# The handover from attention to the first expert: two weight pieces, one copy and a row split put elsewhere

## The chip, the cores and the metric

The kernel runs on one core of one Trainium2 chip. The metric is device time in microseconds (us), as the median over runs of the whole program. The engines are PE (matrix products, with PEld for its weight loads), DVE (vector), ACT (scalar), POOL (GpSimd) and SP (which here only issues DMAs).

## What is computed

The reference is causal attention in a window of 64 positions (8 batches, 8 heads, 576 positions, head size 64), whose output rows (4608 tokens of 512) go through a mixture of 8 experts of which each token uses at most one:

```python
attn = softmax(mask(q @ k.T / 8)) @ v             # window of 64, causal
x = attn.transpose(0, 2, 1, 3).reshape(4608, 512)
do = x @ w_skip > 0                               # the other tokens stay x
e = argmax(x @ w_gate); g = softmax(x @ w_gate)[e]
out = x + g * (relu(x @ w1[e]) @ w2[e])           # where do
```

## The kernel before

**Attention.** The tokens are taken in 36 tiles of 128 (`NT`). For a tile t, `score` makes the scores on PE, `lessen` subtracts the maximum on DVE, `raise_e` is the exponential on ACT, `transpose_p` turns the result on PE and copies it out (`ptm`) on ACT, and `tile_out` multiplies by v (`av`), divides on DVE and stores the rows. The loop at L1182 covers tiles 0 to 34; what follows it (L1226 to L1286) drains the last tiles by hand while the first expert begins. The last tile, 35, is a tail tile: its v lies in `vt`, and `tail_lower(3, 1)` (L372, called at L1244) copies one block of v into place, 64 x 592 numbers on ACT.

**Routing.** The tiles are routed in groups of 8, 8, 6, 6 and 8 (`GRP`). The fourth group (tiles 22 to 27) and the last one (28 to 35) are what the change touches. For the last group `vector_part` (L427) splits the rows on DVE: sums of the gate values (`lg`), their maximum (`gmx`), the difference `gd` (L438), the chosen expert and the bf16 one-hot `gohb`, which PE multiplies with a triangle (`pr`, L513 and L516). `enter` and `one_hots` (L538, L574) then make list entries: some ten small operations on POOL (L581 to L591), two wider ones (L595, L596), a comparison on DVE (L600), two products on POOL (L611), then the list product `lp` on PE (L556). These are generators. `routes(1)` (L765) moves the first generator of queue `late` (the row split) one step on, then the first of queue `later` (the entries). At the marks "sums" and "lists" a generator is held for a count of calls, given by `HOLD`.

**Experts.** A weight piece is 128 x 1024 numbers of float32. SP loads it into one of 6 raw buffers (8 from L1299 on), `weight_hi` rounds it on ACT (`whi`), `weight_lo` subtracts (`wlo = raw - whi`, two inputs in SBUF, 128 x 1024), and the raw buffer is free again. Products are made of three terms (`mm3`). Pieces are counted from 0 here: 0, 1, 2 and 4 are the first expert's four quarters of w1, and 3, 5, 7 and 9 those of w2; 6 and 8 are the second expert's first two quarters of w1. Pieces 0, 1 and 2 are converted by hand, their `wlo` on POOL; all later ones in `weights_to`, on ACT and DVE. A raw buffer is loaded again by the next `weight_dma` in SP's order, which waits until the `wlo` that read it is done.

**Chunks.** `expert_chunks` cuts the products into chunks, and `expert_chunk` first converts weights and then issues the next chunk. With U for w1 and D for w2, a digit for the quarter and a, b for its halves, the chunks are: U0a, U0b, end; U1a, U1b, end; U2a, U2b, D0a, D0b, end; U3a, U3b, D1a, D1b, end; U4a, U4b, D2a, D2b, end; and so on (U4 is the second expert's). "End" chunks issue no products. A U chunk is 12 products into one of two PSUM buffers `p`, then `hh` on ACT and `hl` on DVE (L984, L987), which frees the buffer: so U1b needs the `hl` of U0b, U2a that of U1a, U2b that of U1b. A call of `routes(1)` follows each chunk. U2b and U3a also turn the second item's rows (L895).

**Order.** The kernel is scheduled by hand (`manual_schedule`): each engine takes its instructions in the order in which the program issues them. Before U0a the order is: tail copy on ACT, tile 34's output, turn of tile 35, piece 1 high and low, U0a, tile 35's output, piece 2 high and low, `routes`. Within a chunk the conversions come ahead of `hh` and `hl`. `need` at L1266 is what the next step uses; while routing goes on (`late`, `later` or `side` not empty), `weights_to` converts up to `need` at the first chunk of a step (two pieces together from piece 4 on).

Of the kernel before, what the change touches and what calls it, by code (L numbers as in the profile page):

```python
# [18 lines left out]
B, H, S, HD = 8, 8, 576, 64  # L19
# [3 lines left out]
NT = N // P  # L23
# [33 lines left out]
RATE = 1  # L57
# [1 line left out]
BOTH = 20  # L59
WAIT = {28: 6}  # L60
LWAIT = 8
HOLD = {"sums": 4, "lists": 4}

NXG = 9
CLOSED = 4 * S + 512
# [78 lines left out]
def window_attention_moe(ctx: ExitStack, tc, a, out):  # L144
    nc = tc.nc
# [12 lines left out]
    lists = dram.tile([LROWS, 2], I32, name="lists")  # L158
# [112 lines left out]
    def raise_e(t):  # L271
        s = ss[t]
        nc.scalar.activation(s, s, AF.Exp, scale=0.125)  # L273
# [13 lines left out]
    vms = {}  # L287
# [30 lines left out]
    def keep_busy(n):  # L318

        idle = pav.tile([P, 2, 512], F32, name="av")  # L320
        for _ in range(n):
            nc.tensor.matmul(
                idle[:, 0], onesb, onesb.unsqueeze(1).to_broadcast([P, 4, P]),
                start=True, stop=True, skip_group_check=True,
            )
# [44 lines left out]
        vs[9 * m + 8] = [vt[:, 0], vt[:, 1]]  # L370

    def tail_lower(m, z):  # L372
        nc.scalar.copy(vms["t", m][0][:64, z], vms[4 * m + 2 * z + 1][64:, 3])

    def av_tile(t, lh, sums, av=None):
        blks = tiles[t]
# [50 lines left out]
    def vector_part(t0, n, lh):  # L427
        lg = sm.tile([P, n, 9], F32, name="lg")
        nc.vector.tensor_reduce(lg, lh, axis=AX.X, op=ALU.add)
        l8 = lg[:, :, 0:E]  # L430
        sk = lg[:, :, E]
        g = nc.vector
        bc = lambda z: z.unsqueeze(2).to_broadcast([P, n, E])
        bn = lambda z: z.unsqueeze(1).to_broadcast([P, n, E])
        mx = sm.tile([P, n], F32, name="gmx")
        nc.vector.tensor_reduce(mx, l8, axis=AX.X, op=ALU.max)
        d = sm.tile([P, n, E], F32, name="gd")
        g.tensor_tensor(d, l8, bc(mx), op=ALU.subtract)  # L438
        yield
        fi = sm.tile([P, n, E], F32, name="gfi")  # L440
        nc.vector.scalar_tensor_tensor(fi, d, 0.0, bn(cf[:, off["rev"]]), op0=ALU.is_equal, op1=ALU.mult)
        nd = sm.tile([P, n], F32, name="gnd")
        nc.vector.scalar_tensor_tensor(
            nd, sk, 0.0, cf[:, off["oob"]][:, t0 : t0 + n], op0=ALU.is_le, op1=ALU.mult
        )
        ex = sm.tile([P, n, E], F32, name="gex")
        nc.scalar.activation(ex, d, AF.Exp)
        fm = sm.tile([P, n], F32, name="gfm")
        nc.vector.tensor_reduce(fm, fi, axis=AX.X, op=ALU.max)
        oh = sm.tile([P, n, E], F32, name="goh")  # L450
        nc.vector.tensor_tensor(oh, fi, bc(fm), op=ALU.is_equal)
        ohb = sm.tile([P, n, E], BF16, name="gohb")
        nc.vector.scalar_tensor_tensor(ohb, bc(sk), 0.0, oh, op0=ALU.is_gt, op1=ALU.mult)
        gs = sm.tile([P, n], F32, name="gs")
        nc.vector.tensor_reduce(gs, ex, axis=AX.X, op=ALU.add)
        g.tensor_scalar(gs, gs, 1e-9, None, op0=ALU.add)
        yield "sums"
        return nd, ohb, gs
# [253 lines left out]
    side, pace = [], [None]  # L712

    def drip():
        if side:
            job = side.pop(0)
            if job:
                job[0](*job[1:])
# [36 lines left out]
    late = []  # L755

    later = []
    held, held2 = [None, 0], [None, 0]

    def step(queue, h):  # L760
        h[:] = next(queue[0], queue), 0
        if h[0] is queue:
            queue.pop(0)

    def routes(n):  # L765

        for _ in range(n):
            for queue, h in ((late, held), (later, held2)):
                if not queue:
                    continue  # L770
                if h[0] in ("sums", "lists"):
                    h[1] += 1
                    if progress[0] < NT or h[1] < HOLD[h[0]] + (h is held2 and len(late)):
                        continue
                step(queue, h)

    def sums():
        step(late, held)
# [22 lines left out]
    progress = [0]  # L801

    steps = [(i, qi) for i in range(len(ITEMS)) for qi in range(NQ)]
    part = lambda k, w: (ITEMS[steps[k][0]][2], steps[k][1], w)
# [7 lines left out]
    when = {pc: n for n, pc in enumerate(pieces)}  # L812
    ring, used = [], {}
# [14 lines left out]
    RING = 9  # L828
    ptr = {"dma": 0, "split": 0, "free": 0, "use": 0}
    wrow = {}  # L830

    def weight_dma(n):
        e, qi, w = pieces[n]
        if e not in wrow:
            r = e % E
            ix = perm[0:1, r : r + 1] if r < 2 else tables["order"][0:1, r : r + 1]
            wrow[e] = nc.values_load(ix, engines=[SP], min_val=0, max_val=(E - 1) * NQ * P)
        raw_of[n] = idle.pop(0)
        nc.sync.dma_start(
            raw_of[n], a["wq"][bass.ds(wrow[e] + qi * P, P), w * 1024 : w * 1024 + 1024]  # L840
        )
# [5 lines left out]
    def weight_hi(n):  # L847
        nc.scalar.copy(ring[n % RING][0], raw_of[n])  # L848

    def weight_lo(n, by):  # L850
        hi, lo = ring[n % RING]
        by.tensor_tensor(lo, raw_of[n], hi.bitcast(F32), op=ALU.subtract)  # L852
        if not held_raw(n):
            idle.append(raw_of.pop(n))

    def weight_split(n):
        weight_hi(n)
        weight_lo(n, nc.vector)

    def weights_to(n):  # L860
        n = min(n, len(pieces), ptr["free"] + len(ring))
        while ptr["split"] < n:
            while ptr["dma"] < len(pieces) and idle:
                if not can_load(ptr["dma"]):
                    break
                weight_dma(ptr["dma"])
                ptr["dma"] += 1
            if ptr["dma"] == ptr["split"]:
                break
            weight_split(ptr["split"])  # L870
            ptr["split"] += 1
        while ptr["dma"] < len(pieces) and idle and can_load(ptr["dma"]):
            weight_dma(ptr["dma"])
            ptr["dma"] += 1
# [3 lines left out]
    def can_load(n):  # L878
        return pieces[n][0] % E < 2 or "order" in tables
# [259 lines left out]
    with tc.manual_schedule():  # L1139
# [31 lines left out]
        for m in range(B // 2):  # L1171
            z = 2 * (m == 0)
# [9 lines left out]
        for t in range(NT - 1):  # L1182
            m, r = divmod(t, 9)
            for f, n in at.get(t, ()):
                f(n)
            score(t + 1)
            gates = gate_at.get(t, ())
            if t == 0:
                keep_busy(5)
            for f, n in gates:  # L1190
                f(n)
            if t in (1, 2):
                transpose_p(t - 1)
            routes(1)
            if t != 3:
                lessen(t)
            raise_e(t)
            if t == 2:
                lessen(3)
            if BOTH <= t < NT - 3:  # L1200
                drip()
            if t >= 2:
                tile_out(t - 2)
            for f, n in after_at.get(t, ()):
                f(n)
            if t == NT - 2:
                weight_lo(0, nc.gpsimd)
            if t != NT - 3:
                drip()
            routes(1)  # L1210
            if t > 2:
                transpose_p(t - 1)
            if t == 1:
                clear_rows()
            if t == 7:
                load_constants()
            if t == 10:
                set_constants()
            routes(1)
            for f, n, j in lower_at.get(t, ()):  # L1220
                f(n, j)
            for _ in range(U0.count(t)):
                weight_dma_first()
            if t == NT - 3:
                weight_hi(0)
# [15 lines left out]
        pxs.append(psum.tile([P, 2, 2 * P], F32, name="px", tag="t", bufs=2))  # L1241
        turn_half(its[0].xg, pxs[1], 1)
        split_high(xhl[0][0], pxs)
        tail_lower(B // 2 - 1, 1)  # L1244
        drip()
        drip()
        split_low(*xhl[0], pxs)
# [1 line left out]
        tile_out(NT - 2, last_av)  # L1249
        routes(1)  # L1250
        transpose_p(NT - 1, turned)
        weight_hi(1)
        weight_lo(1, nc.gpsimd)
        scoring.close()
        moe = ExitStack()
        ml = moe.enter_context(tc.tile_pool(name="ml", bufs=1, reuse_waits="tile"))
        ring_slots(ml, 5 - NEARLY)
        hpool["h"] = ml
        chunks = expert_chunks()
        place = [0]  # L1260
        ptr["split"] = 2

        def expert_chunk():
            k = place[0]
            last = len(steps) - 1
            need = max(when[part(min(k + 1, last), 0)], when[part(min(k - 1, last), 1)] if k else 0) + 1  # L1266
            rate = 0 if late or later or side else RATE
            weights_to(max(need, min(ptr["split"] + rate, ptr["free"] + min(RING, len(ring)) - 1)))
            place[0], c = next(chunks)

        expert_chunk()
        drip()
        tile_out(NT - 1)
        weight_hi(2)
        weight_lo(2, nc.gpsimd)
        ptr["split"] = 3
        routes(1)
        pscore.close()
        banks["late"] = ctx.enter_context(tc.tile_pool(name="plate", bufs=1, space=PSUM, reuse_waits="tile"))
        for _ in range(2):  # L1280
            expert_chunk()
            routes(1)
            drip()
        attn.close()
        pattn.close()
        banks["v"] = ctx.enter_context(tc.tile_pool(name="plv", bufs=1, space=PSUM, side="right", reuse_waits="tile"))  # L1286
# [124 lines left out]
        while True:  # L1411
            k = place[0]
# [93 lines left out]
```

## Time and profile before

| what | us |
|---|---|
| median of 3 runs | 409.39 (408.86 to 409.62) |
| the profiled execution | 410.42 |
| its span, first to last instruction | 408.6 |
| PE busy / DVE busy / POOL busy in the span | 391.6 / 305.1 / 154.2 |

The profile is one execution; its rows give start and duration of each instruction in us from the span's start. "[1.30 <-DVE hl L987]" behind a row means that the engine stood idle for 1.30 us before it and that what came last was `hl`. Rows of the same kind that follow each other are merged (x2: two instructions, their stretch together). A PE row of several products overlaps the next row, since matmuls are pipelined.

### The profile page before, as it was taken

To read this page: it belongs to the slowest core of one execution; us is meant where nothing else is said; L and a number is where in the kernel's file an instruction comes from. 1 tells how busy PE (TensorE), PEld (TensorE's weight loads), DVE (VectorE), ACT (ScalarE), POOL (GpSimd) and SP (SyncE) were. 2 spreads that over 40 slices of the span, in tenths; PEclk is the share of its full clock that TensorE was granted. 3 is DMA by queue.
4 is the path that set the end of the run, shared out by engine and by line. 5 is a ranking of instruction groups with operands and counts; after the bars stand their busy time and mean duration, and the time that the engine had idled before them with its cause. 6 is when DMAs were issued, how large, how long until landed. Compare 5 with 4: busy or idle time off the path is not lost.

```text
span 408.6 us, 11475 instructions
## 1 busy us (share of the span) xinstructions
PE 391.6 (96%) x4624; PEld 327.7 (80%) x4624; DVE 305.1 (75%) x537; ACT 218.4 (53%) x373; POOL 154.2 (38%) x276
## 2 busy tenths in 40 slices
PE   8999999999999988899999999999999999999894
PEld 4777777787877778788888989988888888887773
DVE  3788799899899897999468698474375576758771
ACT  1778777866876786354243553442353544533440
POOL 5121368258568687976205042040043030100010
PEclk9999999999999999999999999999999999999898
DMA  8999999999994986847407959454337786642500
GB/s 296 406 400 373 407 408 404 412 389 367 394 341 161 303 280 212 268 157 227 147 2 221 352 161 298 150 181 146 104 117 232 256 276 209 232 135 71 186 31 23
DMA packets 34600, 99.41 MB, mean 243 GB/s; under 512 B 4368, under 2 KB 5648, under 8 KB 34544
## 3 DMA queue, kind: packets, MB, share of 16 engines
q1 hardware_dynamic: 30480, 87.30, 60.7%
q0 software_dynamic: 3200, 9.58, 6.8%
q10 hardware_dynamic: 864, 1.77, 1.1%
q8 instruction: 37, 0.61, 0.6%
q14 instruction: 19, 0.16, 0.1%
HBM read 84.57 MB, written 14.39 MB: 242 GB/s over the span
## 4 chain that ended last, share of the span: by engine, by line
PE 49%; issue 21%; DMA 12%; POOL 8%; DVE 6%; ACT 2%; SPq 1%; POOLq 1%; DVEq 0%
PE av L384 6%; DMA out<-yo,les 5%; PE p L921 5%; PE p L922 4%; PE p L923 4%; PE pt L281 4%; PE ps L252 4%; DMA vT<-vT 2%; DMA gid<-gid 2%; PE yw L921 2%; PE yw L922 2%; PE yw L923 2%; PE yv L921 2%; PE yv L922 2%; PE yv L923 2%
## 5 line engine op out<-in xcount | busy, mean ns | idle before, releaser
L852 DVE TENSOR_TENSOR wlo<-raw,whi 128x1024 fp32r<-128x1024 f32 x69 | 85.5, 1246 | 16.1 <-ACT whi L848 15.9
L984 ACT ACTIVATE hh<-p 128x256 fp32r<-128x256 f32 (+4 forms) x56 | 22.9, 409 | 97.0 <-PE p L923 92.8
L848 ACT CAST whi<-raw 128x1024 fp32r<-128x1024 f32 x72 | 74.4, 1044 | 0.0
L1024 POOL DMA_INDIRECT out<-yo,les x18 | 17.6, 976 | 146.3 <-DVE yo L1015 136.6
L921 PE MATMUL p<-xp,whi 128*128 128x256 f32 (+4 forms) x192 | 58.2, 303 | 1.0 <-DVE hl L987 1.0
L987 DVE SCALAR_TENSOR_TENSOR hl<-p,hh 128x256 fp32r<-128x256 f32 (+4 forms) x56 | 25.2, 451 | 44.7 <-ACT hh L984 33.0
L922 PE MATMUL p<-xp,whi 128*128 128x256 f32 (+4 forms) x192 | 57.0, 297 | 0.0
L923 PE MATMUL p<-xp,wlo 128*128 128x256 f32 (+4 forms) x192 | 56.8, 296 | 0.0
L273 ACT ACTIVATE s<-s 128x1024 f32<-128x1024 f32 x36 | 38.1, 1058 | 27.3 <-DVE s L268 27.1
L267 DVE TENSOR_REDUCE mx<-ps 128x8 f32<-128x1024 f32 x36 | 43.6, 1212 | 6.3 <-PE ps L252 6.3
L268 DVE TENSOR_TENSOR s<-ps,mx 128x1024 f32<-128x1024 f32 x36 | 44.1, 1225 | 4.8 <-PE pt L281 0.3
L384 PEld LDWEIGHTS av<-vm,ptm 128*64 128x64 f32 x992 | 34.3, 136 | 8.8 <-issue 5.9
L384 PE MATMUL av<-vm,ptm 128*64 128x74 f32 x992 | 39.0, 230 | 0.1
L921 PEld LDWEIGHTS p<-xp,whi 128*128 128x128 f32 x192 | 36.2, 188 | 3.7 <-DVE hl L987 1.4
L281 PE MATMUL pt<-gid,s 128*128 128x128 f32 x280 | 38.4, 279 | 0.1
L282 ACT COPY ptm<-pt 128x512 f32<-128x512 f32 x70 | 37.4, 581 | 1.4 <-PE pt L281 1.0
L922 PEld LDWEIGHTS p<-xp,whi 128*128 128x128 f32 x192 | 36.1, 188 | 0.7
L923 PEld LDWEIGHTS p<-xp,wlo 128*128 128x128 f32 x192 | 36.1, 188 | 0.0
L252 PE MATMUL ps<-k,q 64*64 64x128 f32 x1024 | 33.5, 269 | 0.0
L281 PEld LDWEIGHTS pt<-gid,s 128*128 128x128 f32 x280 | 30.1, 141 | 3.1 <-issue 0.4
L353 POOL COPY vm<-vm 64x1184 f32<-64x1184 f32 (+1 forms) x17 | 18.8, 1108 | 35.4 <-ACT vm L351 34.5
L252 PEld LDWEIGHTS ps<-k,q 64*64 64x64 f32 x1024 | 30.2, 133 | 2.1
(240 smaller groups left out, 826.1 us busy)
## 6 DMA issues: line engine op xcount, KB each, us to landing
raw<-wq SPq DMA_DIRECT2D x72, 512.0 KB, 4.7
vm<-vp SPq DMA_DIRECT2D x16, 592.0 KB, 8.2
vT<-vT SPq DMA_DIRECT2D x16, 512.0 KB, 7.6
out<-x SPq DMA_DIRECT2D x32, 256.0 KB, 6.2
q<-qT SPq DMA_DIRECT2D x13, 512.0 KB, 8.1
k<-kT SPq DMA_DIRECT2D x8, 640.0 KB, 8.1
k<-kT SPq DMA_DIRECT2D x7, 512.0 KB, 6.8
kt<-kT SPq DMA_DIRECT2D x8, 256.0 KB, 6.8
```

The costliest lines, as they stand in the source:

```text
L252: nc.tensor.matmul(ps[64 * hf : 64 * hf + 64, r, p], q[h, p], k[h, :, p], start=False, stop=p == 3, skip_group_check=True,)
L267: nc.vector.tensor_reduce(mx, flat, axis=AX.X, op=ALU.max)
L268: pace[0] = nc.vector.tensor_tensor(s, flat, mx.unsqueeze(2).to_broadcast([P, 8, P]), op=ALU.subtract)
L273: nc.scalar.activation(s, s, AF.Exp, scale=0.125)
L281: nc.tensor.transpose(pt[:, p], s[:, 4 * r + p], ident)
L282: nc.scalar.copy(ptm[:, 4 * r : 4 * r + 4], pt)
L384: nc.tensor.matmul(av[64 * hf : 64 * hf + 64, h // 4, (h % 4) * VW : (h % 4 + 1) * VW], ptm[:, (h % 2) * 4 + h // 2, 64 * hf : 64 * hf + 6 ...
L848: nc.scalar.copy(ring[n % RING][0], raw_of[n])
L852: by.tensor_tensor(lo, raw_of[n], hi.bitcast(F32), op=ALU.subtract)
L921: nc.tensor.matmul(o, lh, rh, start=first, stop=False, skip_group_check=parts)
L922: nc.tensor.matmul(o, lh, rl, start=False, stop=False, skip_group_check=parts)
L923: nc.tensor.matmul(o, ll, rh, start=False, stop=last, skip_group_check=parts)
```

## The change

- `weight_hi(1)` takes the place that the tail copy had on ACT, and `weight_lo(1)` goes to DVE behind tile 34's output.
- `weight_hi(2)` and `weight_lo(2)` (still POOL) are issued ahead of U0a, no longer behind tile 35's output.
- `tail_lower(3, 1)` goes to POOL, behind `weight_lo(0)` in the loop's last pass.
- In `vector_part` the difference `gd` moves behind the `yield`, into the next step: it is issued after U0b's `hl`.
- `routes` ends after the step that brings the row split to "sums", so that the entries take no step in that call; the call behind the first "end" chunk is left out; `HOLD["sums"]` is 3 in place of 4.
- While routing goes on, `expert_chunk` converts one piece at every second chunk of a step, as many as `need` asks, and at the least what the step itself uses.

```diff
-HOLD = {"sums": 4, "lists": 4}
+HOLD = {"sums": 3, "lists": 4}
     def tail_lower(m, z):
-        nc.scalar.copy(vms["t", m][0][:64, z], vms[4 * m + 2 * z + 1][64:, 3])
+        to, of = vms["t", m][0][:64, z], vms[4 * m + 2 * z + 1][64:, 3]
+        if m < B // 2 - 1 or z == 0:
+            nc.scalar.copy(to, of)
+        else:
+            nc.gpsimd.tensor_copy(to, of)
...
         nc.vector.tensor_reduce(mx, l8, axis=AX.X, op=ALU.max)
+        yield
         d = sm.tile([P, n, E], F32, name="gd")
         g.tensor_tensor(d, l8, bc(mx), op=ALU.subtract)
-        yield
...
                 step(queue, h)
+                if progress[0] == NT and held == ["sums", 0]:
+                    break
...
                 weight_lo(0, nc.gpsimd)
+                tail_lower(B // 2 - 1, 1)
...
         split_high(xhl[0][0], pxs)
-        tail_lower(B // 2 - 1, 1)
+        weight_hi(1)
...
         transpose_p(NT - 1, turned)
-        weight_hi(1)
-        weight_lo(1, nc.gpsimd)
+        weight_lo(1, nc.vector)
...
-        place = [0]
-        ptr["split"] = 2
+        place, turn = [0], [0, 0]
+        weight_hi(2)
+        weight_lo(2, nc.gpsimd)
+        ptr["split"] = 3
...
+            if k != turn[0]:
+                turn[:] = k, 0
             need = max(when[part(min(k + 1, last), 0)], when[part(min(k - 1, last), 1)] if k else 0) + 1
-            rate = 0 if late or later or side else RATE
-            weights_to(max(need, min(ptr["split"] + rate, ptr["free"] + min(RING, len(ring)) - 1)))
+            if late or later or side:
+                now = max(when[part(min(k, last), 0)], when[part(k - 2, 1)] if k > 1 else 0) + 1
+                weights_to(max(now, min(need, ptr["split"] + (turn[1] % 2 == 0))))
+            else:
+                weights_to(max(need, min(ptr["split"] + RATE, ptr["free"] + min(RING, len(ring)) - 1)))
+            turn[1] += 1
             place[0], c = next(chunks)
 
         expert_chunk()
         drip()
         tile_out(NT - 1)
-        weight_hi(2)
-        weight_lo(2, nc.gpsimd)
-        ptr["split"] = 3
         routes(1)
...
-        for _ in range(2):
-            expert_chunk()
-            routes(1)
-            drip()
+        expert_chunk()
+        routes(1)
+        drip()
+        expert_chunk()
+        drip()
```

## Rows read from the trace of the kernel before

**Rows 1.** Windows: us, busy time PE, PEld, DVE, ACT, POOL, clock, DMA.
```profile
158.40:186.70 28.30, 24.84 (x180) 22.25 (x177) 26.11 (x52) 12.49 (x21) 23.09 (x36) 1.00 0.64 209
186.70:362.00 175.30, 175.21 (x1156) 153.96 (x1155) 116.49 (x195) 76.23 (x129) 40.70 (x35) 1.00 0.60 194
```

**Rows 2.** Waits of PE from 150 to 186: us in total, times, longest.
```profile
PE p L921 <- DVE hl L987: 2.8, 3, 1.3
PE lp L556 <- POOL xg L611: 0.7, 2, 0.4
```

**Rows 3.** Timeline of PE: start, us, what, idle time before and its end.
```profile
162.96 0.39 PE L921 MATMUL p<-xh,whi 128*128 128x256 f32 x1 [1.30 <-DVE hl L987]
...
164.50 0.20 PE L513 MATMUL pr<-gohb,trib 128*128 128x64 bf16 x1
...
165.43 0.39 PE L921 MATMUL p<-xh,whi 128*128 128x256 f32 x1 [0.53 <-DVE hl L987]
...
166.96 0.32 PE L921 MATMUL p<-xh,whi 128*128 128x256 f32 x1
...
169.48 0.44 PE L556 MATMUL lp<-xg,xg 128*128 128x160 bf16 x4 [0.42 <-POOL xg L611]
...
181.78 0.39 PE L921 MATMUL p<-xp,whi 128*128 128x256 f32 x1 [0.96 <-DVE hl L987]
...
183.29 0.73 PE L556 MATMUL lp<-xg,xg 128*128 128x160 bf16 x8
```

**Rows 4.** Timeline of DVE around the first expert.
```profile
158.00 0.42 DVE L987 SCALAR_TENSOR_TENSOR hl<-p,hh 128x256 fp32r<-128x256 f32 x1 [1.57 <-ACT hh L984]
...
160.94 1.63 DVE L438 TENSOR_TENSOR gd<-lg,gmx 128x64 f32<-128x64 f32 x1
162.50 0.41 DVE L987 SCALAR_TENSOR_TENSOR hl<-p,hh 128x256 fp32r<-128x256 f32 x1
...
163.33 0.25 DVE L451 TENSOR_TENSOR goh<-gfi,gfm 128x64 f32<-128x64 f32 x1
...
164.09 0.95 DVE L600 TENSOR_TENSOR xg<-cf,gk 128x768 bf16<-128x768 f32 x1
164.95 0.42 DVE L987 SCALAR_TENSOR_TENSOR hl<-p,hh 128x256 fp32r<-128x256 f32 x1
165.29 1.22 DVE L852 TENSOR_TENSOR wlo<-raw,whi 128x1024 fp32r<-128x1024 f32 x1
...
170.05 2.46 DVE L852 TENSOR_TENSOR wlo<-raw,whi 128x1024 fp32r<-128x1024 f32 x2
...
177.77 3.61 DVE L852 TENSOR_TENSOR wlo<-raw,whi 128x1024 fp32r<-128x1024 f32 x2
```

**Rows 5.** Timeline of POOL in the same stretch.
```profile
157.76 4.74 POOL L852 TENSOR_TENSOR wlo<-raw,whi 128x1024 fp32r<-128x1024 f32 x2 [1.20 <-ACT whi L848]
...
167.37 0.71 POOL L596 TENSOR_SCALAR xg<-xg 128x192 f32<-128x192 f32 x1
168.16 1.95 POOL L611 TENSOR_TENSOR xg<-xg,vals 128x640 bf16<-128x640 f32 x2
170.06 1.37 POOL L533 TENSOR_TENSOR gds<-gds,gohb 128x64 f32<-128x64 f32 x1
...
178.66 3.85 POOL L611 TENSOR_TENSOR xg<-xg,vals 128x640 bf16<-128x640 f32 x2
```

**Rows 6.** Timeline of ACT: tail copy, last tile's turn, piece 1, and U0b's `hh`.
```profile
154.37 0.69 ACT L373 COPY vt<-vm 64x592 f32<-64x592 f32 x1
155.53 0.59 ACT L282 COPY ptm<-turned 128x512 f32<-128x512 f32 x1 [0.48 <-PE turned L281]
...
156.63 1.05 ACT L848 CAST whi<-raw 128x1024 fp32r<-128x1024 f32 x1
...
160.16 0.38 ACT L984 ACTIVATE hh<-p 128x256 fp32r<-128x256 f32 x1 [1.26 <-PE p L923]
```

**Rows 7.** Groups of POOL by form: the like of the moved copy.
```profile
L353 POOL COPY vm<-vm 64x592 f32<-64x592 f32 x2 | 1.3, 670 | 8.9 <-ACT vm L351 8.9
```

## The prediction

> **What bounds the kernel now.** Read the windows first: from 186.7 to 362 PE is busy for 175.21 of 175.30 us, at full clock; in the 28.3 us before that, 158.4 to 186.7, it is busy for 24.84, and DVE for 26.11 [rows 1]. So a microsecond by which the products of the first expert end sooner is carried to the end, as long as the work behind it (loads, conversions, row gathers, which are chained to PE through `hl` and `wlo`) comes along; and PE's idle 3.46 us of that stretch are all that there is to gain there. The waits name them: 2.8 us in three waits for `hl` on DVE, 0.7 in two for the entries' products on POOL [rows 2]. The timeline of PE places them: 1.30 before U1b at 162.96, 0.53 before U2a at 165.43, 0.42 and the rest of the 0.7 at the list product at 169.48, 0.96 before U4b at 181.78 [rows 3].
>
> DVE's timeline then says why [rows 4]. U1b needs the `hl` of U0b. Its `hh` is written by 160.54 [rows 6], but DVE first does `gd`, 64 numbers a partition, for 1.63 us; an operation of that shape takes 0.25 (`goh`). `gd` ends at 162.57, and POOL's two `wlo`, which began at 157.76 and took 4.74, end at 162.50 [rows 4, 5]. The other way round, POOL's `L533` on 64 numbers took 1.37 from 170.06, when DVE's two `wlo` began at 170.05 [rows 4, 5]. So an operation of DVE with two inputs in SBUF and one of POOL wait for each other's end. The Trainium skill has this as a rule (SBUF — State Buffer, Who interferes with whom): a DVE instruction with two SBUF inputs contends with a GpSimd one that reads SBUF, whichever starts first holds the port for the whole instruction, and a `tensor_reduce` never contends. The rows above agree; what the rule says against this change is taken up in the rivals.
>
> **Piece 1.** One `wlo` leaves POOL (half of 4.74, 2.37) and one comes to DVE (1.22 by the row at 165.29). DVE stood idle for 1.57 before 158.00 [rows 4], that is from 156.43, just where it is put; it ends about 157.65, ahead of the `hl` of U0a. Cost: nothing; without that cover it would be up to 1.2 on the `hl` chain. `weight_hi(1)` on ACT takes the place of the tail copy, 1.05 against 0.69; started at 154.37 it ends at 155.42, and ACT's next operation began only at 155.53, after 0.48 of waiting [rows 6].
>
> **Piece 2.** `weight_hi(2)` now stands where `weight_hi(1)` stood, ahead of U0a's `hh`, so ACT is unchanged there. POOL starts that `wlo` when it had started piece 1's, 157.76, and ends at 160.1 in place of 162.50; if DVE's new `wlo` holds up the small row operations of group four ahead of it, by up to 1.2 later, 161.3. On SP the load into the raw buffer of piece 2 now stands ahead of the store of tile 35, which then waits for POOL until 160 to 161; nothing reads those rows before the gathers of the third item, behind the second list product.
>
> **Tail copy on POOL.** 0.67 us for its like [rows 7], behind piece 0's `wlo`. Behind it on POOL stand the second item's two gathers, read first by the turn after U2b, and the row sums of group four. Tile 35's v is there four microseconds ahead of its use. Cost between 0 and 0.67 on POOL, none on PE.
>
> **`gd` behind the `hl` of U0b.** That `hl` now starts at 160.94, where `gd` had, and ends at 161.35. PE came free at 161.66 (162.96 less 1.30) [rows 3], so U1b starts there: 1.30 gained. Even if `gd` still meets POOL's `wlo`, it no longer stands ahead of this `hl`.
>
> **Up to U2a.** U1b to the triangle product takes 1.54 (162.96 to 164.50), that product 0.40 (to 165.43 less 0.53): PE is at 163.20 and 163.60. On DVE `hl`, `gd` at 0.25, the rest of the split (164.09 less 162.50 less 0.34, in which an `hl` makes room for the next, as from 164.95 to 165.29: 1.25) end at 160.94 + 0.34 + 0.25 + 1.25 = 162.78, since the entries' comparison no longer follows in that step. The `hl` of U1a then ends at 163.20 [rows 4], so U2a starts at 163.60 without a wait: 0.53 more. Gained so far 1.83. HOLD at 3, with one call left out, puts the triangle product in the same place, behind U1b.
>
> **U2b, a new wait.** The comparison (0.86 to the next start), piece 3's `wlo` (1.22) and the `hl` of U1b (0.42) now stand behind that `hl`: 163.12 + 0.86 + 1.22 + 0.42 = 165.62 [rows 4]. U2a ends at 163.60 + 1.53 = 165.13 [rows 3]. So U2b waits 0.49; if POOL's L596 (0.71 [rows 5]) gets in between, 1.20. I take 0.7, between the two, because POOL reaches L595 and L596 about when DVE reaches the comparison, and DVE may well be first. Gain at U2b: 1.13.
>
> **First list product.** The entries' steps come one chunk later and the product two chunks later, behind D0b. POOL starts them at about 161 in place of 162.58 and needs, as before, some 7.5 us (162.5 to 170.11 [rows 5]), to 168.5; D0b ends at about 170.7. The 0.67 of waiting goes; below nothing is excluded, as the product itself only moves. Gain 1.80.
>
> **Spread conversions.** Of pieces 4 to 9 the second of each pair comes two chunks later. Before U4b the `hl` of U3b stood behind both of pieces 6 and 7, which took 3.61 in place of 2.46 because POOL's two products (3.85) ran against them [rows 4, 5]. Now piece 6 alone is ahead of it: it is done by about 176.2, U4b starts about 178.5. The 0.96 goes. Gain 2.76. What is late next is piece 7 for D2a: behind the last group's comparison, with one POOL product of about 1.0 let through, I get its end at 180.1 and D2a at 180.4; and the second list product at 181.9, whose POOL part ends about 181.1. Both margins are below 1, so each may cost between 0 and 1.0; I take 0, as POOL and DVE both begin their part earlier than before.
>
> **Sum.** 1.30 + 0.53 - 0.70 + 0.67 + 0.96 = 2.76, say 2.8. The profiled execution took 410.42 with a span of 408.6 (1.8 lies around it); it is 1.0 above the median. Its like would take 407.6; from the median 409.39 the forecast is **406.6**. Bounds: U2b's wait at 0.49 gives 406.4; at 1.20 with 0.5 lost at D2a or the second list product 407.6. The forecast's own range is 406.1 to 407.7.
>
> **Rivals.**
> - *The port keeps DVE the bound* (408.0, chance 0.17). The rule of the Trainium skill above would have it so: the two engines still take turns, only elsewhere. From the rows: DVE has 26.11 busy of 28.3 and 2.2 idle [rows 1]; if only `gd`'s excess (1.63 less 0.25, 1.4) is saved and every other excess comes back with another partner, the stretch can shrink by 1.4. For: DVE is busier than PE there. Against: the excess in `wlo` (1.15) came from two conversions back to back.
> - *More than forecast* (405.6, 0.05): no wait at U2b, and other products start closer together; 3.46 idle plus small change.
> - *The waits come back* (409.4, 0.08): U2b at 1.20, D2a and the second list product 1.0 each leave 0.3, too little to measure. This is also where it ends if the edits move waits and remove none.
> - *Slower, by piece 7 too late* (410.6, 0.06). Before, piece 7 was ready at 181.38 and D2a followed U4b and the list product at 183.8. Now it stands right ahead of the product that needs it. If it ends after 183.8, three microseconds later than I get, all is lost, and each further turn of POOL's 1.0 on DVE is a loss; two such turns and a late pair of pieces 10 and 11 (1.2 more, since they are converted together once routing is over) give 1.2 slower. Against: POOL would have to be let in four times.
>
> **Chances.** Forecast 0.64, rivals as above. The range 405.7 to 408.7 takes in the forecast's own, the first and second rival's, and leaves out about 0.17. A measurement of this kernel can tell about 0.2%, 0.8 us, from no change: faster by more 0.85, within 0.09, slower 0.06.
>
> **What would show it.** Right: `gd` at about 0.25 behind `hl`; no idle time before U1b, U2a, the first list product and U4b; some 0.5 to 1 before U2b; D-chunks of the first expert some 2 us earlier, and PE dense from about 184. Wrong: `gd` or another small DVE operation above 1 us on the way to an `hl`; waits before D2a or the second list product; or new idle time behind 184, above all for a `hl` behind pieces 10 and 11, which would mean that the gain of this stretch is given back.

## The result and the profile after

| what | before | after |
|---|---|---|
| median, runs of one chip (us) | 409.50 (408.81 to 410.37, 6 runs) | 405.92 (405.52 to 406.51, 6 runs) |
| ratio, 95% interval | | 0.9915 [0.9900, 0.9931] |
| the profiled execution / its span | 410.42 / 408.6 | 405.84 / 404.1 |

The change gains 3.58 us, 0.85%; the forecast was 2.8. A second measurement of the same kernel on another chip (`after_again`, below) gave less, 2.87 by its medians, with a ratio of 0.9936 [0.9915, 0.9958]. The windows come first, as in [rows 1]: us, busy time of PE, PEld, DVE, ACT, POOL, clock, DMA, here of the kernel after, with the later edges moved roughly with the work.

```profile
158.40:183.70 25.30, 24.66 (x184) 22.44 (x183) 22.61 (x48) 11.29 (x19) 20.47 (x34) 1.00 0.72 237
183.70:357.50 173.80, 173.71 (x1145) 152.37 (x1145) 116.80 (x195) 76.61 (x130) 42.98 (x37) 1.00 0.60 197
```

PE's idle time in the first stretch fell from 3.46 [rows 1] to 0.64, by 2.82; behind 183.7 PE is as dense as before. The waits of PE from 158 to 200 (us in total, times, longest) have one line left:

```profile
PE p L927 <- DVE hl L993: 0.6, 1, 0.6
```

The timeline of PE after (start, us, what, idle time before and its end) answers to [rows 3]. From the top: U0a, U1b, the triangle product, U2a, U2b, U3a, U4b, the second list product, and the third item's first turn, behind the end of the stretch.

```profile
155.21 0.36 PE L927 MATMUL p<-xh,whi 128*128 128x256 f32 x1
...
160.96 0.28 PE L927 MATMUL p<-xh,whi 128*128 128x256 f32 x1
...
162.40 0.20 PE L517 MATMUL pr<-gohb,trib 128*128 128x64 bf16 x1
...
162.68 0.38 PE L927 MATMUL p<-xh,whi 128*128 128x256 f32 x1
...
165.02 0.38 PE L927 MATMUL p<-xh,whi 128*128 128x256 f32 x1 [0.64 <-DVE hl L993]
...
170.17 0.36 PE L927 MATMUL p<-xh,whi 128*128 128x256 f32 x1
...
177.77 0.28 PE L927 MATMUL p<-xp,whi 128*128 128x256 f32 x1
...
181.97 0.73 PE L560 MATMUL lp<-xg,xg 128*128 128x160 bf16 x8
...
195.32 0.49 PE L901 MATMUL px<-gid,xg 128*128 128x128 f32 x3
```

The rows of the kernel before that [rows 3] lacks for the comparison, from its timeline of PE: U0a, the product of U1a that first reads piece 1's `wlo`, the last product ahead of U1b's wait, U1b's second product (the first is in [rows 3]), U3a, and the third item's first turn.

```profile
155.64 0.36 PE L921 MATMUL p<-xh,whi 128*128 128x256 f32 x1
...
160.21 0.39 PE L923 MATMUL p<-xh,wlo 128*128 128x256 f32 x1
...
161.39 0.28 PE L923 MATMUL p<-xh,wlo 128*128 128x256 f32 x1
...
163.19 0.28 PE L922 MATMUL p<-xl,whi 128*128 128x256 f32 x1
...
173.13 0.28 PE L921 MATMUL p<-xh,whi 128*128 128x256 f32 x1
...
199.31 0.49 PE L895 MATMUL px<-gid,xg 128*128 128x128 f32 x3
```

From start to start the two traces compare like this (us; the forecast is the prediction's term, each taken from an idle row):

| from, to | before | after | gained | forecast |
|---|---|---|---|---|
| U0a to U1b | 7.32 | 5.75 | 1.57 | 1.30 |
| U1b to U2a | 2.47 | 1.72 | 0.75 | 0.53 |
| U2a to U2b | 1.53 | 2.34 | -0.81 | -0.70 |
| U2b to U3a (first list product within) | 6.17 | 5.15 | 1.02 | 0.67 |
| U3a to U4b | 8.65 | 7.60 | 1.05 | 0.96 |
| U4b to the third item's turn | 17.53 | 17.55 | -0.02 | 0 |
| sum | 43.67 | 40.11 | 3.56 | 2.76 |

The sum is the difference of the medians (3.58) to 0.02, which is closer than two executions of one kernel agree: in `after_again` the way from U0a to the third item's turn took 41.66, a gain of 2.01. The spans differ by 4.5, and the rest belongs to these two executions. U0a stood 0.43 earlier from work ahead of the change. Near the end the clock of PE differed: in the kernel before the granted clock fell to 0.73 and then 0.50, the level of 1.2 GHz, from 380 to 384, and in the kernel after the same work, four microseconds earlier, was done at 1.00. The windows (columns as above; before, then after):

```profile
380.00:382.00 2.00, 1.35 (x7) 1.35 (x7) 1.34 (x5) 1.17 (x2) 0.00 (x0) 0.73 0.28 91
382.00:384.00 2.00, 2.00 (x8) 1.71 (x7) 1.93 (x4) 0.45 (x2) 0.00 (x0) 0.50 0.00 0
```
```profile
376.00:380.00 4.00, 3.28 (x30) 2.46 (x30) 3.27 (x8) 1.60 (x4) 0.00 (x0) 1.00 0.14 47
```

The shift between the two traces is 3.99 at the third item's turn, still 3.98 ahead of these windows (the product at 380.65 before and 376.67 after), and 4.42 at PE's last product (402.80 and 398.38). So what the change gained was carried to the end, and 0.44 came on top there. Why the clock fell in the one execution and not in the other is not shown.

DVE's timeline after answers to [rows 4]: piece 1's `wlo`, U0b's `hl`, `gd`, the comparison, piece 3's `wlo`, the `hl` of U1b and of U2a, and piece 7's `wlo`.

```profile
155.84 1.22 DVE L858 TENSOR_TENSOR wlo<-raw,whi 128x1024 fp32r<-128x1024 f32 x1
...
160.39 0.41 DVE L993 SCALAR_TENSOR_TENSOR hl<-p,hh 128x256 fp32r<-128x256 f32 x1
160.72 0.21 DVE L443 TENSOR_TENSOR gd<-lg,gmx 128x64 f32<-128x64 f32 x1
...
162.54 0.95 DVE L604 TENSOR_TENSOR xg<-cf,gk 128x768 bf16<-128x768 f32 x1
163.41 1.22 DVE L858 TENSOR_TENSOR wlo<-raw,whi 128x1024 fp32r<-128x1024 f32 x1
164.54 0.75 DVE L993 SCALAR_TENSOR_TENSOR hl<-p,hh 128x256 fp32r<-128x256 f32 x2
...
176.73 1.41 DVE L858 TENSOR_TENSOR wlo<-raw,whi 128x1024 fp32r<-128x1024 f32 x1
```

`gd` takes 0.21 where it took 1.63 [rows 4], and stands behind the `hl`. POOL's timeline after answers to [rows 5]: the moved copy, a small sum, piece 2's `wlo`, an operation on 6 numbers, and the two pairs of entry products.

```profile
152.56 0.67 POOL L377 COPY vt<-vm 64x592 f32<-64x592 f32 x1 [0.44 <-DMA xg<-out,es]
...
156.03 1.16 POOL L537 TENSOR_TENSOR gds<-gds,gohb 128x48 f32<-128x48 f32 x1
...
158.32 2.40 POOL L858 TENSOR_TENSOR wlo<-raw,whi 128x1024 fp32r<-128x1024 f32 x1
...
163.63 1.05 POOL L595 TENSOR_TENSOR gl<-gl,vals 128x6 f32<-128x6 f32 x1
...
166.28 2.72 POOL L615 TENSOR_TENSOR xg<-xg,vals 128x640 bf16<-128x640 f32 x2
...
177.62 2.87 POOL L615 TENSOR_TENSOR xg<-xg,vals 128x640 bf16<-128x640 f32 x2
```

Piece 2's `wlo` ends at 160.72, ahead of `gd`'s row; the small operations that DVE's `wlo` holds up are now POOL's (1.16 and 1.05), and PE waits for none of them.

### The profile page after: what moved, and what is told of

Same layout as the page of the kernel before. It is cut to its first block, busy times and chain, and to the rows that moved or that the text cites. A ratio compares the mean times of both kernels' runs of the same rounds, so it can differ in the third digit from the quotient of the medians.

```text
span 404.1 us, 11475 instructions
## 1 busy us (share of the span) xinstructions
PE 389.3 (96%) x4624; PEld 325.4 (81%) x4624; DVE 303.6 (75%) x538; ACT 217.7 (54%) x372; POOL 154.8 (38%) x276
## 4 chain that ended last, share of the span: by engine, by line
PE 54%; issue 19%; DMA 12%; DVE 7%; POOL 5%; ACT 2%; SPq 1%; POOLq 0%; DVEq 0%
PE av L388 7%; PE p L927 5%; DMA out<-yo,les 5%; PE pt L281 5%; PE p L928 5%; PE p L929 5%; PE ps L252 4%; PE yw L927 2%; PE yw L928 2%; PE yw L929 2%; DMA gid<-gid 2%; PE yv L927 2%; PE pw L331 2%; PE yv L928 2%; PE yv L929 2%
## 5 line engine op out<-in xcount | busy, mean ns | idle before, releaser
L858 DVE TENSOR_TENSOR wlo<-raw,whi 128x1024 fp32r<-128x1024 f32 x70 | 86.5, 1240 | 16.2 <-ACT whi L854 16.0
L273 ACT ACTIVATE s<-s 128x1024 f32<-128x1024 f32 x36 | 38.1, 1058 | 27.4 <-DVE s L268 27.1
```

## The experiments

A ratio is to the kernel before on the same chip. Its median was 409.70 beside `gd_back`, `entries_back`, `pairs_back` and `odd_turns`, 411.03 beside `one_on_pool`, `gd_only`, `spread_only` and `tail_back`, 410.45 beside `late_three` and `after_again`, and 410.03 beside `both_back`; so times of different sets are compared by their ratios. "The distance" is the time from the last exponential (ACT L273) to the third item's first turn: 47.50 before, 43.88 after. In the second execution of the kernel after (`after_again`) it was 44.90, so a distance alone tells nothing below 1 us, and verdicts rest on the waits as well.

**What freed U1b.** Three kernels undo one of the two reasons, or both: POOL done earlier (piece 1 on DVE), and `gd` behind the `hl`.

`gd_back`, the kernel after with

```diff
-        yield
         d = sm.tile([P, n, E], F32, name="gd")
         g.tensor_tensor(d, l8, bc(mx), op=ALU.subtract)
+        yield
```

> The changed kernel with one part undone: gd is issued ahead of the hl of U0b again. If the gain before U1b came from POOL letting the port go earlier (its wlo of piece 2 ended at 160.72, gd would start at about 160.4), gd takes 0.3 to 0.6 us, U1b waits less than 0.7, and the time is 406.3 (405.9 to 406.8; changed kernel 405.9). If the order of gd and hl is what counted, gd is again above 1 us, U1b waits 1.3, and the time is about 407.4.

Measured: 406.17, ratio 0.9912 [0.9895, 0.9928], distance 43.85. `gd` began at 162.14 and took 0.30, for POOL's `wlo` (159.96, 2.40) ended at 162.36. There was no idle row before U1b, and 0.47 before U2b. With POOL done early the order of `gd` costs a quarter of a microsecond at most (U1a to U1b took 1.68, after 1.43).

`one_on_pool`, the kernel after with

```diff
-        weight_lo(1, nc.vector)
+        weight_lo(1, nc.gpsimd)
```

> The changed kernel with piece 1's wlo on POOL again, ahead of piece 2's. POOL's two then end at about 161.7, gd (from 160.7) waits for the port to 161.7, and the hl of U1a and everything DVE does behind it come 0.9 later: U2a and U2b 0.9 later, 406.7 (406.3 to 407.1). If it is enough that gd stands behind the hl of U0b, 405.9.

Measured: 408.37, ratio 0.9918 [0.9888, 0.9948], distance 44.90. Apart from a later start the trace is as expected: POOL's two `wlo` (158.87, 4.75) ended at 163.62 and `gd`, behind the `hl`, took 1.04, to 163.70. U1b had no idle row, but the triangle product waited 0.30, U2a 0.33, U2b 0.64, and from U1b's start U2a came 0.98 later than after. The distance equals that of `after_again` and the interval takes in the kernel after, so the size is not settled by this run.

`both_back` undoes both.

> The kernel after with two of its parts undone together: gd stands ahead of U0b's hl again, and piece 1's wlo is on POOL again. Each part alone undone left U1b without an idle row (gd met POOL's wlo for 0.30 and 1.04 us, in the one case because POOL had only one wlo left, in the other because gd stood behind the hl). If either of the two is enough and the pair is what frees U1b, gd now meets the first of two wlo on POOL again, takes about 1.6 us ahead of the hl, and U1b waits about 1.3 as before; the other parts keep their gains (no wait at U4b, list products without a wait). From U0b's start to the third item's first turn 38.9 to 39.5 us (after 37.3 and 38.0 in two executions, one_on_pool alone 38.6, before 40.9); time about 407.4. If U1b's wait had another cause, that distance stays at 37.3 to 38.6, the time at 406 to 406.7.

Measured: 407.73, ratio 0.9939 [0.9918, 0.9960], from U0b to the third item's turn 38.83, 0.07 below what was expected. The ratio is that of `after_again` (0.9936), so the verdict rests on the rows. From its timelines of PE, DVE and POOL:

```profile
162.90 0.39 PE L927 MATMUL p<-xh,whi 128*128 128x256 f32 x1 [1.29 <-DVE hl L993]
```
```profile
161.19 1.32 DVE L442 TENSOR_TENSOR gd<-lg,gmx 128x64 f32<-128x64 f32 x1
162.44 0.41 DVE L993 SCALAR_TENSOR_TENSOR hl<-p,hh 128x256 fp32r<-128x256 f32 x1
```
```profile
157.70 4.73 POOL L858 TENSOR_TENSOR wlo<-raw,whi 128x1024 fp32r<-128x1024 f32 x2
```

The wait of before is back (1.29, [rows 3] 1.30), with `gd` ending just behind POOL's `wlo`, at 162.51 and 162.43. So either part alone frees U1b from this wait.

`gd_only` makes the other test, the kernel before with `gd`'s move alone.

> The kernel before with one part of the change alone: gd is issued behind the hl of U0b. By the prediction's accounting the 1.30 before U1b is gained and kept: 408.0 or less. The other reading: POOL's wlo still ends at 162.5, gd (now from 161.3) still waits for it, the rest of the split, the comparison and the hl of U1a end at about 165.1, and the list product still waits for POOL: U1b starts at 161.5, U2a at about 165.1 and D0a as before; 409.4 (409.0 to 409.7).

Measured: 411.08, ratio 0.9995 [0.9973, 1.0017], distance 47.36. U1b's wait is gone and no gain is measured. From its timelines of PE and DVE:

```profile
161.68 0.39 PE L923 MATMUL p<-xh,wlo 128*128 128x256 f32 x1 [0.55 <-POOL wlo L852]
...
165.16 0.19 PE L513 MATMUL pr<-gohb,trib 128*128 128x64 bf16 x1 [0.58 <-DVE gohb L453]
...
166.72 0.39 PE L921 MATMUL p<-xh,whi 128*128 128x256 f32 x1 [1.19 <-DVE hl L987]
```
```profile
162.42 1.64 DVE L439 TENSOR_TENSOR gd<-lg,gmx 128x64 f32<-128x64 f32 x1
```

`gd` is as long as before (1.64), and what stands behind it, the triangle product and U2a, waits in U1b's place. U1a's 0.55 is a wait for piece 1's `wlo`, which POOL began only at 159.23 in this execution. So the order alone moves the wait; POOL's earlier end removes it.

**Entries one chunk later.** `entries_back`, the kernel after with

```diff
-HOLD = {"sums": 3, "lists": 4}
+HOLD = {"sums": 4, "lists": 4}
...
-                if progress[0] == NT and held == ["sums", 0]:
-                    break
...
-        expert_chunk()
-        routes(1)
-        drip()
-        expert_chunk()
-        drip()
+        for _ in range(2):
+            expert_chunk()
+            routes(1)
+            drip()
```

> The changed kernel with one part undone: HOLD 4, no break in routes, and the call behind the first end chunk is back, so the entries' comparison stands ahead of the hl of U1a and the first list product behind U2b again. If the place of the entries carries part of the gain, U2a waits about 0.9 and the list product about 2 us for POOL's two products, which ended at 169.0: 408.0 (407.3 to 408.5). If it does not matter, 405.9 to 406.2.

Measured: 406.92, ratio 0.9934 [0.9917, 0.9952], distance 44.65. Its timeline of PE has waits at U2a and at the first list product, and none at U2b:

```profile
163.29 0.39 PE L925 MATMUL p<-xh,whi 128*128 128x256 f32 x1 [1.08 <-DVE hl L991]
...
167.34 0.44 PE L560 MATMUL lp<-xg,xg 128*128 128x160 bf16 x4 [0.42 <-POOL xg L615]
168.03 0.30 PE L560 MATMUL lp<-xg,xg 128*128 128x160 bf16 x2 [0.25 <-POOL xg L615]
```

The two waits of before are there, U2a's longer; less U2b's 0.64 the idle rows are 1.1 more than after. So the place of the entries carries part of the gain, as expected, but less of it: the list product waited 0.67 and not 2, since POOL's two products ended at 167.98, earlier too, and the time of 406.9 lies below the expected range from 407.3.

**Spread conversions.** `pairs_back`, the kernel after with

```diff
-            if late or later or side:
-                now = max(when[part(min(k, last), 0)], when[part(k - 2, 1)] if k > 1 else 0) + 1
-                weights_to(max(now, min(need, ptr["split"] + (turn[1] % 2 == 0))))
-            else:
-                weights_to(max(need, min(ptr["split"] + RATE, ptr["free"] + min(RING, len(ring)) - 1)))
+            rate = 0 if late or later or side else RATE
+            weights_to(max(need, min(ptr["split"] + rate, ptr["free"] + min(RING, len(ring)) - 1)))
```

> The changed kernel with one part undone: from piece 4 on two pieces are again converted together at the first chunk of a step. By the prediction's accounting the 0.96 before U4b comes back, with what a restart costs 1.1: 407.0. The other reading is that the last group's comparison, which now stands behind the hl of U3b, was the larger part of that delay: then the hl of U3b ends by about 177 and the time is 406.1 (405.8 to 406.4).

Measured: 406.21, ratio 0.9911 [0.9896, 0.9927], distance 43.95. U4b does not wait although pieces 6 and 7 are converted together again. Its timeline of DVE, ahead of U4b:

```profile
175.56 2.36 DVE L858 TENSOR_TENSOR wlo<-raw,whi 128x1024 fp32r<-128x1024 f32 x2 [0.26 <-ACT whi L854]
177.84 0.42 DVE L993 SCALAR_TENSOR_TENSOR hl<-p,hh 128x256 fp32r<-128x256 f32 x1
178.17 1.31 DVE L604 TENSOR_TENSOR xg<-cf,gk 128x1024 bf16<-128x1024 f32 x1
```

The two `wlo` take 2.36, not 3.61 [rows 4], and the last group's comparison stands behind the `hl`: the entries came one chunk later, POOL's products (now from 180.29) no longer run against that pair. In this order U4b does without the spread.

`spread_only`, the kernel before with the spread alone (the same lines the other way round).

> The kernel before with one part of the change alone: one piece at every second chunk. The wait of 0.96 before U4b should go, with what a restart costs 1.1: 408.4 (408.2 to 408.8). If the last group's comparison and POOL's products hold DVE up as long without the second wlo, 409.3.

Measured: 410.01, ratio 0.9974 [0.9954, 0.9994], distance 46.72. U4b's wait is gone, 0.15 at the second list product is new, and the waits at U1b, U2a and the first list product (1.30, 0.54, 0.42 with 0.25) stand as before. The gain of 1.02 by the medians is the one expected. So the spread does remove that wait in the old order; in the new one the order has done so already. With neither, in the kernel before and in `gd_only`, the wait stands (0.96 and 0.97).

`odd_turns` moves each conversion by one chunk, the kernel after with `(turn[1] % 2 == 1)` in place of `== 0`.

> The changed kernel with the conversions at every odd chunk of a step in place of every even one: piece 3's wlo then stands behind the hl of U1b. If the wait of 0.64 before U2b is that wlo's alone, it goes, with what a restart costs 0.8 in all: 405.1 (404.8 to 405.5). If DVE is the bound by now, the wait comes back before a later U chunk, at the latest behind pieces 10 to 12: 405.9.

Measured: 406.98, ratio 0.9937 [0.9918, 0.9957], distance 43.70. In its timeline of PE, U2b's wait is gone and has come back in front of the products that need piece 7 and a later one:

```profile
179.16 0.50 PE L928 MATMUL yw<-wlo,hh 128*128 128x512 f32 x1 [0.45 <-DVE wlo L858]
...
188.58 0.39 PE L929 MATMUL p<-xp,wlo 128*128 128x256 f32 x1 [0.16 <-DVE wlo L858]
```

The time lies above both expected values (405.1 and 405.9): from U4b to the third item's turn this kernel needed 18.61, the kernel after 17.55. This is the danger that the prediction named for piece 7, here by one chunk.

**The tail copy.** `tail_back`, the kernel after with the copy on ACT in its old place, ahead of `weight_hi(1)`:

```diff
-        if m < B // 2 - 1 or z == 0:
-            nc.scalar.copy(to, of)
-        else:
-            nc.gpsimd.tensor_copy(to, of)
+        nc.scalar.copy(to, of)
...
-                tail_lower(B // 2 - 1, 1)
...
         split_high(xhl[0][0], pxs)
+        tail_lower(B // 2 - 1, 1)
         weight_hi(1)
```

> The changed kernel with the tail copy back on ACT, ahead of weight_hi(1). The last tile's turn would then be copied out 0.4 later and hh of U0a 0.45 later; U0a's products cover the first, and DVE's 0.38 and 0.23 of idle time the second: 406.0 (405.8 to 406.3). If ACT has no room for it, the last tile's av starts 0.5 to 0.7 later and all behind it: 406.6.

Measured: 407.89, ratio 0.9918 [0.9884, 0.9952], distance 43.97. No worth of the copy's place shows, but the interval is wide: about 1.4 us to either side, with the kernel after (0.9915) inside. In this execution the last tile's `av` took 1.49 and U0a to U0b 3.04, after 1.26 and 2.78, so some 0.25 was not covered there. U2b waited 0.95 here, but so it did, by 0.96, in `after_again`.

**The wait that is left.** `late_three` moves piece 3 alone behind the `hl` that U2b needs:

```diff
-                weights_to(max(now, min(need, ptr["split"] + (turn[1] % 2 == 0))))
+                weights_to(max(now, min(need, ptr["split"] + (turn[1] % 2 == (k == 1)))))
```

> The kernel after, with piece 3's two conversions moved from the first chunk behind the first end (ahead of U1a's and U1b's hl) to the second one, behind the hl that U2b needs; pieces from 4 on stay where the change puts them. After, U2b waited 0.64 for the hl of U1b, with that wlo (1.22 us) on the way to it. If the wlo alone makes that wait, and the work behind 184 us is not bound by DVE, the wait goes with its drain and restart (0.64 and 0.25 less what PE then meets next, about 0.8): from the last exponential to the third item's first turn 43.1 to 43.4 us in place of 43.9, time about 405.2 beside 405.9 for the kernel after. If DVE's chain of conversions and hl is what sets the end of that stretch, the wait comes back in front of a later product that needs piece 3 (D0a is first) or a later hl, and the distance stays at 43.7 to 44.0, the time at 405.9.

The kernel after ran beside it:

> The kernel after, unchanged, as the measure for the other run of this call on the same chip: 405.9 us, 0.9915 of the kernel before, distance from the last exponential to the third item's first turn 43.7 to 44.0 us.

Measured: `late_three` 406.90 (5 runs), ratio 0.9908 [0.9894, 0.9922], distance 44.50; `after_again` 407.58 (8 runs), 0.9936 [0.9915, 0.9958], 44.90. The timeline of DVE in `late_three`: the comparison, U1b's `hl`, piece 3.

```profile
164.00 0.95 DVE L604 TENSOR_TENSOR xg<-cf,gk 128x768 bf16<-128x768 f32 x1
164.87 0.42 DVE L993 SCALAR_TENSOR_TENSOR hl<-p,hh 128x256 fp32r<-128x256 f32 x1
165.41 1.23 DVE L858 TENSOR_TENSOR wlo<-raw,whi 128x1024 fp32r<-128x1024 f32 x1
```

From 158 to 200 its PE has no idle row. So piece 3's `wlo` made U2b wait, and DVE behind it is not the bound: no wait comes back by 200. U2a to U2b took 1.54, after 2.34; of these 0.80 some 0.5 are left at the third item's turn (from U1b's start 33.85, the kernel after 34.36 and 34.78). From U0b to that turn it needs 37.10, the kernel after 37.33 and 38.02. The medians differ by 0.7, near the 0.8 expected, but the two intervals overlap; that this version is faster than the kernel after is likely, not settled. Neither distance met its number, for both executions lost time ahead of U0b (last section).

## Why the prediction was right, and where it was not

**What bounds the kernel: right.** All of the gain lies between U0a and U4b, and it was carried on: from U4b to the third item's turn the two traces need the same time (17.53 and 17.55), and the shift between them is still 3.98 near 380. Only the sentence that PE's idle 3.46 were all there was to gain was too low: 3.56 were gained although U2b's new 0.81 is in the sum.

**Size of the waits: the step that was off.** The forecast took each wait at its idle row, in all 2.76; the starts give 3.56. The wait before U1b shows why. Products start 0.12 apart (160.72, 160.84, 160.96 in the trace after), but each row lasts 0.28: ahead of that wait the last one began at 161.39 and counts as busy to 161.67, 0.16 after the next could have begun. So 1.30 of idle delayed U1b by 1.45. Behind the wait the second product follows the first by 0.23 (162.96 to 163.19), not 0.12, and this 0.11 falls into the table's next line. The Trainium skill says (Perfetto Trace Analysis, Tensor Engine Instruction) that a product's row starts with the prefetch of its data and that its end is estimated from its size and a delay; rows of 0.28 that start 0.12 apart agree with that. In the five lines the starts give 0.09 to 0.35 more than the idle rows.

A short wait leaves no row at all. The 0.12 that U1b's line has beyond 1.45 reads as one, inside U1a: the product at 160.21, the first to read piece 1's `wlo`, has a row of 0.39 and the next one follows by 0.22, in place of 0.12. POOL's first `wlo` ended just ahead of it (half of 4.74 from 157.76 [rows 5] is 160.13), and in `gd_only`, where POOL began later, the same product has an idle row of 0.55. So piece 1's move to DVE seems to have freed U1a as well (its products start evenly in the trace after), which the prediction did not count. Another is U1b's in `after_again`: it began 0.39 behind the product ahead of it, and the timeline of PE shows nothing idle.

```profile
161.28 0.28 PE L929 MATMUL p<-xh,wlo 128*128 128x256 f32 x1
161.67 0.39 PE L927 MATMUL p<-xh,whi 128*128 128x256 f32 x1
```

How much of this excess stands in the time is open. `after_again` gained 2.87 by the medians, as forecast, but its trace has other losses against the excess: U0a to U0b took 0.86 more than in the first execution, and U2b waited 0.96. That its total meets the forecast is partly luck.

**`gd`, piece 1 and piece 2: right.** Piece 1's `wlo` took 1.22 in DVE's gap, piece 2's ended at 160.72 within 160.1 to 161.3, `gd` took 0.21 and U1b had no wait. The prediction gave the gain to `gd`'s place and left the port as a side matter; `gd_back` and `both_back` show that either would do for U1b, and `gd_only` that the place alone gains nothing that can be measured, since U2a stands behind `gd` too. So the step from `gd`'s place to 1.30 gained and kept holds only together with piece 1's move.

**The port (rival 408.0): not so.** The Trainium skill's rule (SBUF — State Buffer, Who interferes with whom) holds in the trace after: POOL's `L595` on 6 numbers took 1.05 and ended at 164.68, with DVE's `wlo` of 163.41 to 164.63. But the excess fell on operations for which PE does not wait, and DVE's busy time is 22.61 of 25.3. That an excess moves to another partner doesn't mean that it moves to another one on the path. It can, though: in `after_again` POOL's `L599` came first, and piece 3's `wlo`, on the way to U2b's `hl`, took 1.53 in place of 1.22. Its timelines of POOL and DVE:

```profile
163.39 1.29 POOL L599 TENSOR_TENSOR xg<-cf,gc 128x192 f32<-128x192 f32 x1
```
```profile
164.23 1.53 DVE L858 TENSOR_TENSOR wlo<-raw,whi 128x1024 fp32r<-128x1024 f32 x1
```

**U2a and U2b: right.** 0.53 went, and U2b waits 0.64, between the bounds 0.49 and 1.20 and near the 0.70 taken. DVE was first, as argued, and POOL's `L595` was held up, not the `wlo`. The second execution gave 0.96, with that `wlo` at 1.53, so which engine comes first is not fixed, and the upper part of the bounds occurs as well.

**First list product: right.** POOL's part ended at 169.00 (forecast 168.5), the product began at 169.78 behind D0b. `entries_back` brings its 0.42 and 0.25 back.

**U4b: right size, half of the reason.** The 0.96 went, but the spread was not needed for it: `pairs_back` has no wait without it, because the comparison and POOL's products come later. The prediction gave one cause to a wait that two parts of the change each remove. The margins held: piece 7 was ready at 178.14, 1.04 ahead of D2a (forecast 180.1 and 180.4), the second list product had 1.5. `odd_turns` shows that they are real: one chunk later, and 0.45 of idle appears there.

**Slower, by piece 7 too late: not so**, since piece 7 was ready two microseconds earlier than I got.

## What to carry to other kernels

Price a wait from start to start of the work around it, not by its idle row: here a wait was worth its row and 0.1 to 0.35 more, and waits of 0.12 and 0.27 left no row. Moving a blocked operation behind the one that is needed helps only if the next needed one is not behind it too; taking away what blocks it (here one of POOL's two conversions) helps all that follow. When two parts of a change each remove the same wait, undo each alone and both together before giving one of them the gain.

## What the runs showed of the hardware

Between executions of one kernel the handover varies. In `after_again` ACT stood idle for 1.73 ahead of the last tile's turn copy and DVE for 1.65 at about the same time, although the rows of PE on which they wait had ended by 155.03. In `late_three`, `one_on_pool`, `both_back` and `gd_only` ACT's idle time there was 0.93 to 1.57 and DVE's 0.16 to 1.57. The copy in ACT's timeline of `after_again`:

```profile
156.25 0.59 ACT L282 COPY ptm<-turned 128x512 f32<-128x512 f32 x1 [1.73 <-PE pt L281]
```

In the first execution of the same kernel that copy started at 155.10, after 0.24. In `after_again` PE waited 0.43 for it at tile 35's `av`, and U0a to U0b took 3.64, not 2.78. What held the two engines the rows do not show, and no run here was made for it. The wait of PE for the second item's gathers ahead of U0a (0.59 in the first execution after) varied too, from none to 0.85. The distance of the two executions after differs by 1.0 us, as much as most of the single parts tested here are worth.
